# Attention and two dense layers on one core: queries loaded by whole tiles, values by pairs of heads, and all attention loads on ScalarE's queue

## The chip, the cores and the metric

The program runs on one core of a Trainium2 chip. A core has five engines that each work through their own list of instructions in order: TensorE (PE, matrix products), VectorE (DVE), ScalarE (ACT), GpSimd (POOL) and SyncE (SP, which here only starts transfers). Transfers (DMA) are started by an instruction of one of these engines and then run by themselves; an instruction that needs the data waits on a semaphore. The metric is the device time of one execution in microseconds (us); less is better. The kernel before takes 687.59 us, the median of three runs (685.85 to 687.65).

## What is computed

```python
def _attn_ref(q, k, v):                     # 2 batches, 8 heads, 576 positions, 64 wide
    scores = scale * np.matmul(q, k.transpose(0, 1, 3, 2))
    kth = np.partition(scores, -top_k, axis=-1)[..., -top_k:-top_k + 1]   # top_k = 32
    scores = np.where(scores >= kth, scores, -1000000000.0)
    attn = np.exp(scores - np.max(scores, axis=-1, keepdims=True))
    attn = attn / (np.sum(attn, axis=-1, keepdims=True) + 1e-09)
    return np.matmul(attn, v)
...
    x = attention, as 1152 tokens x 512
    h = x @ w_in;  x = (max(h, 0) + log1p(exp(-|h|))) @ w_out           # layer 0, 512 -> 2048 -> 512
    h = x @ w_in2; x = (max(h, 0) + alpha * min(h, 0)) @ w_out2         # layer 1, the same sizes
```

Inputs are float32, but the weights reach the device as 64-bit numbers, which the kernel turns into float32 itself.

## The kernel before

**Tiles.** The 1152 tokens are nine tiles of 128. `CHUNKS` (L35) groups them as [3, 4], [5, 6, 7] and [8, 0, 1, 2]. Tile 4 lies across the two batches, so it has two parts. For each tile and each of its 8 heads there is one row of attention work, 72 in all (`rows`, L377).

**One row of attention.** `scores` (L408) works on a pair of heads: PE forms the products of a query tile `q` with the keys `ks` (L430) and ACT copies them from PSUM to `s`, half a row at a time (L435). `topk` (L445) finds the 32 largest of 576 scores on DVE with four MAX (`best`, L439) and three MATCH_REPLACE (`strike`, L442), then masks and exponentiates with ACT and POOL (L459 to L485; the mask may go to DVE, L478). `flip` (L487) transposes the result on PE, and `values` (L506) multiplies by the values `v` on PE. `finish` (L558) scales a finished tile; its last step writes `xh`, the input of layer 0.

**Weights.** 32 units of 128 x 1024 numbers are turned from 64 bits into float32 by `convert` (L311): a load of 1 MB into `cr` (L317, two buffers), two DVE instructions (L320 and L325), one ACT instruction (L327), four POOL additions (L331) and a store of 512 KB to a scratch tensor `ws` (L334). `fetch` (L352) loads a unit back when a layer needs it (L359).

**Layers.** `Layer.up` (L611) forms `ph` from the tile inputs (L623 for the chunks worked in plain float32, L594 to L596 for the others, as three products of parts), `down` (L655) accumulates `pa` (L671, or again L594 to L596). Between them, for layer 0, ACT and DVE form `g`; its last step is the SCALAR_TENSOR_TENSOR of L638. `ph` has two buffers, so the third `ph` needs the first `g` to be done. Chunk 0 (tiles 3 and 4) goes through layer 0, then layer 1, while attention for chunk 1 is still under way, and so on.

**What sets the order.** Nothing is issued where it is written. Each piece of work is handed to a `Planner` (L97) with an engine, an assumed length and a due time; `order` (L143) lists all pieces engine by engine, always the piece with the earliest due time among those whose inputs are ready by its own estimate. The due times come from constants (`PACE`, `ROWS_DUE`, `AHEAD`, `LOAD_LEAD` and others, L48 to L66). The engines then run these lists in order.

**Loads for attention.** All transfers are in SP's list. Keys come as one load of 288 KB for two heads (`prepare_k`, L397), values as one load of 160 KB for one head (`prepare_v`, L406), and queries as one load of 64 KB for a tile and a pair of heads (L418, inside `scores`). A load into a buffer that is still read waits for PE; everything behind it in SP's list waits too. Transfers also take turns on eight completion semaphores: the ninth cannot be issued before the first has landed, and so on.

Of the kernel before, what the change touches and what calls it, by code (L numbers as in the profile page):

```python
# [19 lines left out]
P = 128  # L20
# [14 lines left out]
CHUNKS = [[3, 4], [5, 6, 7], [8, 0, 1, 2]]  # L35
RING = 4
# [5 lines left out]
QB = 6  # L42
KB = 5
VB = 10
# [3 lines left out]
SPARE = [-17033.9, 2009.0, 903.3]  # L48
MASK_SPARE = [24031.0, 784.7, -18754.5]
# [5 lines left out]
T0 = 229.4  # L55
VALUES = 1.35
SCORES = 0.69
PACE = [1433.1, 1301.1, 6152.8, 6484.8, 326.6, 8896.4]
ROWS_DUE = [(-1910.7, -760.0), (978.8, 846.5), (2800.8, 12532.4)]
EARLY_DUE = [-2160.8, -143.0, 2538.2]  # L60
LOAD_LEAD = 3880.4
FETCH_LEAD = [364.0, 1458.3, -965.3]
EARLY = 24
DIRECT_LEAD = 9718.0
RAW_LEAD = 2408.7
AHEAD = {'scores': [1943.9, 1871.5, 6694.5], 'mask': [46.7, -1169.1, 345.0], 'flip': [12526.4, 4276.2, 25384.6], 'values': [-301.3, 947.9, -2654.2], 'chain': [9471.3, 6009.7, -3110.2], 'split': [1852.9, -2106.4, -15053.3], 'edge': [5637.9, -646.3, 560.8]}  # L66
MASKS = [['act'], ['act'], ['act']]
NATIVE = {(0, 0), (1, 0)}
# [199 lines left out]
def topk_attention_moe_kernel(ctx: ExitStack, tc: tile.TileContext, q, k, v, w1, w2, w3, w4, alpha, out):  # L268
# [4 lines left out]
    plan = Planner()  # L273
    op = plan.op
# [19 lines left out]
    begins = [T0 + sum(PACE[:i]) for i in range(2 * len(CHUNKS))]  # L294
# [6 lines left out]
    def moe_due(ci, layer, j):  # L301
        n = 2 * ci + layer
        return begins[n] + PACE[n] * j / FJ

# [6 lines left out]
    def convert(unit, due):  # L311
# [22 lines left out]
        op("SP", 0.45, due, lambda: nc.sync.dma_start(z, f().bitcast(F32)), reads=[f], writes=[f"ws{nm}"],  # L334
# [65 lines left out]
    def prepare_v(b, h, ci, due):  # L400
        if (b, h) in vst:
# [104 lines left out]
    def values(i):  # L506
# [5 lines left out]
        for b, _, _ in spans(t):  # L512
            prepare_v(b, h - 1, ci, due)
            prepare_v(b, h, ci, due)
# [4 lines left out]
        parts = [((vst[b, h - 1], vst[b, h]), c0, w) for b, c0, w in spans(t)]  # L519

        def products():
            for vts, c0, w in parts:
                o = h // 2 * P + c0
                for c in range(5):
                    for half, vt in enumerate(vts):
                        block = (c + 5 * half if c < 4 else 4) * P + c0
                        nc.tensor.matmul(av()[half * D:(half + 1) * D, o:o + w], vt()[:, c, :], pt[:, block:block + w],
                                         start=c == 0, stop=c == 4)

        op("PE", VALUES * len(parts), due, products, reads=[*pts] + [vt for vts, _, _ in parts for vt in vts], writes=[av],  # L530
# [4 lines left out]
    def features(name, bufs, ci, layer):  # L535

        n = len(CHUNKS[ci]) * P
# [60 lines left out]
    class Layer:  # L598
# [3 lines left out]
        def __init__(self, layer, ci):  # L602
            self.layer, self.ci, self.tiles = layer, ci, CHUNKS[ci]
# [4 lines left out]
            self.turned = layer == 0 and ci == len(CHUNKS) - 1 and not self.native  # L608
# [46 lines left out]
        def down(self, j):  # L655
# [40 lines left out]
            if self.layer == 0:  # L696
# [123 lines left out]
```

## Time and profile before

| | us |
|---|---|
| median of three runs | 687.59 |
| lowest and highest run | 685.85, 687.65 |
| the profiled execution, its own time | 689.61 |
| its span, first to last instruction | 687.7 |
| PE busy | 620.6 (90%) |
| DVE busy | 544.3 (79%) |
| ACT busy | 485.3 (71%) |
| POOL busy | 359.6 (52%) |

The rest of the page divides the span into 40 slices, lists the chain of work that ended last, the costliest groups of instructions, and the transfers. PE's share of the span grows from about half in the first fifth to nearly all of the time afterwards; DVE's is highest in the first half. A busy share over the whole span therefore hides that different engines are full at different times, and the tables by stretch have to be read beside it.

### The profile page before, as it was taken

How to read it: one execution, taken by the hardware profiler on the slowest of the kernel's cores; microseconds unless marked ns; L12 is line 12 of the kernel's file. 1: busy time of each engine (PE TensorE's matmuls, PEld its weight loads, DVE VectorE, ACT ScalarE, POOL GpSimd, SP SyncE). 2: the span in 40 equal slices, each digit the busy share in tenths (PEclk: the TensorE clock that was granted, in tenths of full speed). 3: DMA queues.
4: the chain of work that ended last, by engine and by line, in shares of the span. 5: the costliest groups of instructions: out<-in, count | busy, mean ns of one | idle time of the engine just before them, and what ended most of it. 6: DMA issues, size and time to landing. Idle time of an engine off the chain costs nothing.

```text
span 687.7 us, 10318 instructions
## 1 busy us (share of the span) xinstructions
PE 620.6 (90%) x3432; PEld 463.7 (67%) x3432; DVE 544.3 (79%) x1024; ACT 485.3 (71%) x975; POOL 359.6 (52%) x393
## 2 busy tenths in 40 slices
PE   5746545699999999999999999999999999999997
PEld 3424434466666566568877778878888888788885
DVE  4999999999999899999999999989545544554442
ACT  3877678698869778878888888788675655533431
POOL 0575666565575469766987677868411112121120
PEclk9686655699999999999999999999999999999999
DMA  8877667778978883842332312122142232313121
GB/s 286 283 250 232 196 215 216 239 238 269 305 266 309 248 271 108 269 148 84 123 108 92 106 50 93 62 93 92 62 168 95 91 112 72 121 63 123 61 92 61
DMA packets 34324, 109.59 MB, mean 159 GB/s; under 512 B 3936, under 2 KB 12128, under 8 KB 30176
## 3 DMA queue, kind: packets, MB, share of 16 engines
q1 hardware_dynamic: 34272, 108.94, 47.7%
q8 instruction: 27, 0.44, 0.3%
q14 instruction: 25, 0.20, 0.1%
HBM read 89.79 MB, written 19.14 MB: 158 GB/s over the span
## 4 chain that ended last, share of the span: by engine, by line
PE 67%; DVE 12%; DMA 7%; POOL 5%; issue 4%; ACT 4%; SPq 1%; POOLq 0%; DVEq 0%; ACTq 0%
PE ph L594 8%; PE pa L594 8%; PE pa L596 8%; PE pa L595 8%; PE ph L596 8%; PE ph L595 8%; DMA cr<-in_w_dram 6%; PE pa L671 5%; DVE m L439 4%; PE pss L430 4%; DVE r L442 4%; PE ph L623 4%; PE pp L497 3%; POOL cx L331 3%; DVE cr L325 2%
## 5 line engine op out<-in xcount | busy, mean ns | idle before, releaser
L439 DVE MAX8 m<-r 128x8 f32<-128x576 f32 x216 | 156.2, 747 | 0.4
L481 POOL TENSOR_TENSOR e<-s,e 128x288 f32<-128x288 f32 x144 | 122.6, 862 | 40.1 <-ACT e L476 28.4
L331 POOL TENSOR_TENSOR cx<-cx,cr 128x256 int32<-128x256 int32 x128 | 98.8, 792 | 83.3 <-ACT cr L327 61.5
L343 POOL TENSOR_TENSOR w<-w 128x512 fp32r<-128x512 f32 x68 | 92.3, 1367 | 79.3 <-ACT w L349 75.6
L442 DVE MATCH_REPLACE8 r<-m,r 128x576 f32<-128x576 f32 x144 | 106.4, 741 | 0.0
L343 POOL TENSOR_TENSOR gl<-g,gh 128x384 fp32r<-128x384 f32 (+1 forms) x40 | 46.4, 1160 | 100.6 <-ACT gh L651 100.4
L430 PE MATMUL pss<-ks,q 64*128 64x288 f32 x320 | 75.7, 531 | 19.7 <-ACT s L435 11.9
L327 ACT ACTIVATE cr<-cr 128x1024 int16<-128x1024 uint32 x32 | 80.0, 2500 | 17.4 <-DVE cr L325 17.2
L497 PE MATMUL pp<-ident,e 128*128 128x128 f32 x288 | 48.4, 301 | 34.6 <-ACT e L483 21.9
L349 ACT CAST w<-w 128x1024 fp32r<-128x1024 f32 x64 | 66.9, 1045 | 11.1 <-DMA w<-ws 10.9
L497 PEld LDWEIGHTS pp<-ident,e 128*128 128x128 f32 x288 | 37.1, 153 | 52.7 <-ACT e L483 26.6
L430 PEld LDWEIGHTS pss<-ks,q 64*128 64x128 f32 x320 | 35.5, 219 | 48.8 <-ACT s L435 19.3
L594 PE MATMUL pa<-w,gh 128*128 128x512 f32 x160 | 66.9, 418 | 0.0
L435 ACT COPY s<-pss 128x288 f32<-128x288 f32 x144 | 52.0, 406 | 19.6 <-PE pss L430 15.6
L595 PE MATMUL pa<-w,gl 128*128 128x512 f32 x160 | 63.3, 396 | 0.0
L596 PE MATMUL pa<-w,gh 128*128 128x512 f32 x160 | 63.2, 395 | 0.0
L483 ACT ACTIVATE e<-e,nb 128x576 f32<-128x576 f32 x72 | 55.6, 772 | 9.0 <-POOL e L481 9.0
L344 DVE TENSOR_TENSOR w<-w 128x512 fp32r<-128x512 f32 x60 | 45.1, 787 | 18.6 <-ACT w L349 18.6
L638 DVE SCALAR_TENSOR_TENSOR g<-ph,g 128x256 f32<-128x256 f32 (+2 forms) x48 | 26.6, 554 | 42.1 <-ACT g L637 40.9
L439 DVE MAX8 m<-s 128x8 f32<-128x576 f32 x72 | 53.0, 746 | 8.2 <-ACT s L435 8.0
L442 DVE MATCH_REPLACE8 r<-m,s 128x576 f32<-128x576 f32 x72 | 53.4, 741 | 0.0
L644 DVE SCALAR_TENSOR_TENSOR g<-g,rest,ph 128x256 f32<-128x256 f32 (+2 forms) x48 | 29.2, 608 | 30.4 <-ACT g L642 28.3
(127 smaller groups left out, 1389.2 us busy)
## 6 DMA issues: line engine op xcount, KB each, us to landing
w<-ws SPq DMA_DIRECT2D x88, 512.0 KB, 3.3
cr<-in_w_dram SPq DMA_DIRECT2D x32, 1024.0 KB, 7.4
ws<-cx SPq DMA_DIRECT2D x32, 512.0 KB, 7.6
v<-in_v_dram SPq DMA_DIRECT2D x24, 160.0 KB, 4.3
ks<-in_k_dram SPq DMA_DIRECT2D x12, 288.0 KB, 4.3
q<-in_q_dram SPq DMA_DIRECT2D x40, 64.0 KB, 4.1
out_dram<-o SPq DMA_DIRECT2D x9, 256.0 KB, 2.0
al<-in_alpha_dram SPq DMA_DIRECT2D x1, 8.0 KB, 2.8
```

The source lines that it names most:

```text
L327: op("ACT", ACT_LOW, due, lambda: nc.scalar.activation(raw().bitcast(I16)[:, :, 2], low(), AF.Copy, scale=2.0 ** -29), reads=[f], writes=[ ...
L331: op("POOL", on_pool(cs.stop - cs.start), due, lambda cs=cs: nc.gpsimd.tensor_add(f().bitcast(I32)[:, cs], f().bitcast(I32)[:, cs], high() ...
L343: lambda cs=cs: nc.gpsimd.tensor_sub(lo()[:, cs], x()[:, cs], hi()[:, cs].bitcast(F32)),
L349: op("ACT", on_act(WIDE), due, lambda: nc.scalar.copy(w()[:, 0, :], x()), reads=reads, writes=[w])
L430: nc.tensor.matmul(pss[n](), qr()[n * D:(n + 1) * D, :], ks()[n * D:(n + 1) * D, cs], start=j == 0, stop=j == len(qk) - 1)
L439: op("DVE", on_dve(n), due, lambda: nc.vector.max(out=out(), in_=x()), reads=reads, writes=writes)
L442: op("DVE", on_dve(n) + 0.067, due, lambda: nc.vector.match_replace(out=out(), in_to_replace=found(), in_values=x(), imm_value=LOWEST), re ...
L481: op("POOL", on_pool(HS), due - AHEAD["mask"][ci], lambda cs=cs: nc.gpsimd.tensor_sub(e()[:, cs], s()[:, cs], e()[:, cs]), reads=[s], writ ...
L497: nc.tensor.transpose(pp()[:, c * P:(c + 1) * P], e()[:, c0 + c * P:c0 + (c + 1) * P], ident)
L594: nc.tensor.matmul(acc, ah, b_l, start=first, stop=False)
L595: nc.tensor.matmul(acc, a_l, bh, start=False, stop=False)
L596: nc.tensor.matmul(acc, ah, bh, start=False, stop=last)
```

## The change

Queries are loaded for a whole tile at once (four pairs of heads, 256 KB, ten loads in place of forty, two buffers in place of six). Values are loaded for a pair of heads (320 KB, twelve loads in place of twenty-four, five buffers of double size in place of ten). Keys keep their twelve loads. All 34 of these loads are issued by ACT; SP keeps the weights, the scratch stores, the fetches and the output. The new `STORER` is SP as before, and `TOGETHER` with three groups of one chunk leaves the layers as they were. The planner's constants have new values, so that the order of work on every engine is another one.

```diff
+LOADER = 'ACT'
+STORER = 'SP'
+ISSUE = {"SP": 0.45, "ACT": 0.45, "POOL": 1.0}
-QB = 6
+QB = 2
-VB = 10
+VB = 5
-T0 = 229.4
+T0 = 30.2
-PACE = [1433.1, 1301.1, 6152.8, 6484.8, 326.6, 8896.4]
+PACE = [1198.9, 591.1, 6130.8, 6026.0, 276.5, 3112.4]
...
-        op("SP", 0.45, due + AHEAD["scores"][ci] - LOAD_LEAD, lambda: nc.sync.dma_start(ks(), k[b, pair]), writes=[ks],
-           move=P * S * 4)
+        op(LOADER, ISSUE[LOADER], due + AHEAD["scores"][ci] - LOAD_LEAD, lambda: loader.dma_start(ks(), k[b, pair]),
+           writes=[ks], move=P * S * 4)
...
-        vst[b, h] = vt = buf("v", VB, [P, 5, D], F32, f"v{b}{h}")
-        op("SP", 0.45, due + AHEAD["values"][ci] - LOAD_LEAD / 2, lambda: nc.sync.dma_start(vt(), v[b, h]), writes=[vt], move=P * 5 * D * 4)
+        vst[b, pair] = vt = buf("v", VB, [P, 2, 5, D], F32, f"v{b}{pair}")
+        op(LOADER, ISSUE[LOADER], due + AHEAD["values"][ci] - LOAD_LEAD / 2, lambda: loader.dma_start(vt(), v[b, pair]),
+           writes=[vt], move=P * 10 * D * 4)
+
+    def prepare_q(t, n, ci, due):
+        if (t, n) in qst:
+            return
+        qst[t, n] = qr = buf("q", QB, [P, H // 2, P], F32, f"q{t}_{n}")
+        op(LOADER, ISSUE[LOADER], due + AHEAD["scores"][ci] - LOAD_LEAD, lambda: loader.dma_start(
+            qr(), q[:, NT if n else t]), writes=[qr], move=P * H // 2 * P * 4)
...
-            qr = buf("q", QB, [P, P], F32, f"q{t}{pair}{n}")
-            op("SP", 0.45, due + AHEAD["scores"][ci] - LOAD_LEAD, lambda n=n, qr=qr: nc.sync.dma_start(
-                qr(), q[:, NT if n else t, pair]), writes=[qr], move=P * P * 4)
-            qk.append((qr, kst[b, pair]))
+            prepare_q(t, n, ci, due)
+            qk.append((qst[t, n], kst[b, pair]))
...
-                        nc.tensor.matmul(pss[n](), qr()[n * D:(n + 1) * D, :], ks()[n * D:(n + 1) * D, cs],
+                        nc.tensor.matmul(pss[n](), qr()[n * D:(n + 1) * D, pair, :], ks()[n * D:(n + 1) * D, cs],
...
-            prepare_v(b, h - 1, ci, due)
-            prepare_v(b, h, ci, due)
+            prepare_v(b, h // 2, ci, due)
...
-        "v": vp.reshape(B, H, 5, P, D).transpose(0, 1, 3, 2, 4),
+        "v": vp.reshape(B, H // 2, 2, 5, P, D).transpose(0, 1, 4, 2, 3, 5),
```

What the new order is shows in two places.

**ACT's list, from its start.** In a name, the digits say which part it is: `s30` is tile 3, head 0; `cr010` is a weight unit of layer 0; `ks00` and `v00` are batch 0 and pair 0; `q4_0` is tile 4. DMAHW0 to DMAHW7 are the eight completion semaphores. Before, from the second instruction on:

```order
L282 ACT_TABLE_LOAD
L435 COPY s30_139<-pss300_127 128x288 [waits PE_49]
L435 COPY s31_141<-pss310_129 128x288 [waits PE_49]
L435 COPY s30_139<-pss301_145 128x288 [waits PE_49]
L435 COPY s31_141<-pss311_147 128x288 [waits PE_49]
L459 ACTIVATE nb30_171<-m30_161 128x1 [waits DVE_49]
```

Now, after the table load and the loads of `ks00`, `q3_0`, `ks01`, `ks02` and `ks03`, which wait for nothing:

```order
L421 DMA q4_0_124<-in_q_dram 128x512 [waits DMAHW0_49]
L405 DMA ks10_126<-in_k_dram 128x576 [waits DMAHW1_49]
L414 DMA v00_128<-in_v_dram 128x640 [waits DMAHW2_49]
L414 DMA v01_130<-in_v_dram 128x640 [waits DMAHW3_49]
L414 DMA v02_132<-in_v_dram 128x640 [waits DMAHW4_49]
L414 DMA v03_134<-in_v_dram 128x640 [waits DMAHW5_49]
L414 DMA v10_136<-in_v_dram 128x640 [waits DMAHW6_49]
L335 ACTIVATE cr000_109<-cr000_109 128x1024 [waits DVE_49]
L294 ACTIVATE rest_70<-al_69 128x16
L335 ACTIVATE cr010_113<-cr010_113 128x1024 [waits DVE_49]
L449 COPY s30_158<-pss300_147 128x288 [waits PE_49]
L449 COPY s31_161<-pss310_149 128x288 [waits PE_49]
```

Twelve loads and two weight conversions now stand ahead of the first copy of scores. DMAHW0 is the semaphore of `cr000` and DMAHW2 that of `cr010`, the first two loads in SP's list, which in the kernel before came behind eleven loads of keys and queries. DVE's list begins with L328 and L333 for `cr000` and then for `cr010`, and the first MAX is fifth; before, it was first.

**DVE's list where layer 0 begins.** `xh0` is the input of layer 0 for chunk 0, `g00_0` its first result between the two products. Before:

```order
L581 TENSOR_TENSOR xh0_694<-pav4__748,xn4_1160 128x4x128
L442 MATCH_REPLACE r55_1171<-m55_1133,s55_1082 128x576
L320 TENSOR_SCALAR cx007_1178<-cr007_1114 128x1024
L439 MAX m55_1133<-r55_1171 128x8
L325 TENSOR_SCALAR cr007_1114<-cr007_1114 128x1024
L442 MATCH_REPLACE r55_1171<-m55_1133,r55_1171 128x576
L439 MAX m52_1048<-r52_1056 128x8
L439 MAX m55_1133<-r55_1171 128x8
L442 MATCH_REPLACE r54_1217<-m54_1145,s54_1079 128x576
L442 MATCH_REPLACE r55_1171<-m55_1133,r55_1171 128x576
L320 TENSOR_SCALAR cx017_1229<-cr017_1153 128x1024
L638 SCALAR_TENSOR_TENSOR g00_0_1219<-ph00_0_1174,g00_0_1219 128x256
```

Now:

```order
L594 TENSOR_TENSOR xh0_626<-pav4__711,xn4_1118 128x4x128
L333 TENSOR_SCALAR cr017_1069<-cr017_1069 128x1024
L453 MAX m55_1100<-r55_1120 128x8
L456 MATCH_REPLACE r54_1145<-m54_1111,s54_1056 128x576
L456 MATCH_REPLACE r55_1120<-m55_1100,r55_1120 128x576
L453 MAX m54_1111<-r54_1145 128x8
L453 MAX m55_1100<-r55_1120 128x8
L456 MATCH_REPLACE r54_1145<-m54_1111,r54_1145 128x576
L456 MATCH_REPLACE r55_1120<-m55_1100,r55_1120 128x576
L453 MAX m54_1111<-r54_1145 128x8
L652 SCALAR_TENSOR_TENSOR g00_0_1169<-ph00_0_1138,g00_0_1169 128x256
```

From the list's start to this first `g00_0`, DVE had 84 MAX, 64 MATCH_REPLACE, 16 of L320 and 15 of L325; now it has 86 MAX, 65 MATCH_REPLACE, 16 of L328, 16 of L333 and one mask (L492). On PE the same work stands ahead of the first `ph` of layer 0 in either list: 60 score products, 81 transposes, 120 products with values and 16 that spread the sums. The same holds once more where the first `ph` of chunk 1 begins: 108 score products, 184 transposes and 240 products with values are behind it in either list.

## Rows read from the trace of the kernel before

**Rows 1.** The page: busy tenths in 40 equal slices of the span.

```profile
PE   5746545699999999999999999999999999999997
DVE  4999999999999899999999999989545544554442
```

**Rows 2.** By stretch: start:end length, busy time of engines, clock, DMA share, GB/s.

```profile
0.00:17.20 17.20, 9.02 (x26) 5.60 (x26) 7.73 (x16) 6.52 (x14) 0.70 (x6) 0.97 0.85 286
17.20:141.60 124.40, 73.28 (x492) 49.81 (x492) 120.59 (x236) 93.63 (x183) 78.04 (x97) 0.66 0.72 230
141.60:310.00 168.40, 164.87 (x878) 107.72 (x879) 159.44 (x317) 139.01 (x293) 108.73 (x133) 1.00 0.74 245
310.00:600.00 290.00, 289.94 (x1682) 233.66 (x1681) 219.87 (x407) 213.80 (x443) 158.25 (x151) 1.00 0.28 95
600.00:687.70 87.70, 83.47 (x358) 66.89 (x356) 36.69 (x53) 32.32 (x47) 13.90 (x8) 1.00 0.24 84
...
8.00:13.00 5.00, 4.80 (x14) 2.61 (x12) 2.90 (x7) 2.19 (x7) 0.00 (x0) 1.00 0.97 333
```

**Rows 3.** Timeline where layer 0 begins: start, length, engine, work, [idle before, releaser].

```profile
132.97 0.69 DVE L581 TENSOR_TENSOR xh<-pav__748,xn 128x512 f32<-128x512 f32 x1 [0.30 <-ACT xn L578]
...
141.12 0.41 DVE L638 SCALAR_TENSOR_TENSOR g<-ph,g 128x256 f32<-128x256 f32 x1
...
141.59 1.99 PE L623 MATMUL ph<-xh,w 128*128 128x256 f32 x8 [1.34 <-DVE g L638]
```

**Rows 4.** Timeline of the first 20 us.

```profile
0.74 0.39 SPq L397 DMA_DIRECT2D ks<-in_k_dram  x1
...
5.92 0.90 SPq L317 DMA_DIRECT2D cr<-in_w_dram  x2
...
6.51 1.61 DVE L439 MAX8 m<-s 128x8 f32<-128x576 f32 x2 [6.51 <-ACT s L435]
...
13.77 0.69 DVE L320 TENSOR_SCALAR cx<-cr 128x1024 uint32<-128x1024 uint32 x1 [2.87 <-DMA cr<-in_w_dram]
```

**Rows 5.** Transfers issued near 6 us and near 93 us: KB, us to landing.

```profile
cr<-in_w_dram SPq DMA_DIRECT2D x2, 1024.0 KB, 8.8
...
cr<-in_w_dram SPq DMA_DIRECT2D x1, 1024.0 KB, 5.7
```

**Rows 6.** ACT's groups from 0 to 20 us: xcount, busy us, mean ns.

```profile
L327 ACT ACTIVATE cr<-cr 128x1024 int16<-128x1024 uint32 x2 | 5.0, 2484 | 4.7 <-DVE cr L325 4.7
L435 ACT COPY s<-pss 128x288 f32<-128x288 f32 x12 | 4.4, 406 | 4.9 <-PE pss L430 4.9
```

**Rows 7.** DVE's groups from 0 to 141.1 us (L478: 0 to 297).

```profile
L439 DVE MAX8 m<-r 128x8 f32<-128x576 f32 x62 | 44.6, 744 | 0.0
L442 DVE MATCH_REPLACE8 r<-m,r 128x576 f32<-128x576 f32 x42 | 30.9, 738 | 0.0
L325 DVE TENSOR_SCALAR cr<-cr 128x1024 uint32<-128x1024 uint32 x15 | 12.9, 860 | 0.0
...
L478 DVE TENSOR_SCALAR e<-s,m 128x576 f32<-128x576 f32 x5 | 2.9, 587 | 0.0
```

**Rows 8.** DVE's waits, 17.2 to 141, then 141 to 310 us.

```profile
DVE cx L320 <- DMA cr<-in_w_dram: 3.5, 3, 1.6
...
DVE cx L320 <- DMA cr<-in_w_dram: 4.9, 5, 2.0
```

**Rows 9.** What SP's list waited for, 0 to 297 us: total, times, longest.

```profile
SPq L418 <- PE pss L430: 38.7, 11, 7.6
...
SPq L397 <- PE pss L430: 18.0, 6, 7.1
...
SPq L406 <- PE pav__748 L527: 6.2, 2, 5.1
```

**Rows 10.** What PE waited for, 0 to 141 us.

```profile
PE pss L430 <- DMA q<-in_q_dram: 3.8, 1, 3.8
...
PE pss L430 <- DMA ks<-in_k_dram: 0.7, 1, 0.7
```

More of the change, by code (lines that the diff above doesn't have):

```diff
@@ L47 @@
 OB = 4
-SPARE = [-17033.9, 2009.0, 903.3]
-MASK_SPARE = [24031.0, 784.7, -18754.5]
+SPARE = [-7022.5, 1525.8, -3032.5]
+MASK_SPARE = [945.1, 705.4, -504.7]
 CXB = 3
@@ L273, in topk_attention_moe_kernel @@
     plan = Planner()
+    loader, storer = ({"SP": nc.sync, "ACT": nc.scalar, "POOL": nc.gpsimd}[x] for x in (LOADER, STORER))
     op = plan.op
@@ L293, in topk_attention_moe_kernel @@
     first_row = [sum(len(c) for c in CHUNKS[:i]) * H for i in range(len(CHUNKS) + 1)]
-    begins = [T0 + sum(PACE[:i]) for i in range(2 * len(CHUNKS))]
+    among = {ci: group for group in TOGETHER for ci in group}
+    passes = [(layer, ci) for ci in range(len(CHUNKS)) for layer in (0, 1) if not layer or among[ci][-1] == ci]
+    begins = {p: T0 + sum(PACE[:i]) for i, p in enumerate(passes)}
+    paces = dict(zip(passes, PACE))
     def row_due(i):
@@ L301, in moe_due @@
     def moe_due(ci, layer, j):
-        n = 2 * ci + layer
-        return begins[n] + PACE[n] * j / FJ
+        return begins[layer, ci] + paces[layer, ci] * j / FJ
     mats = {0: (w1, w2), 1: (w3, w4)}
@@ L518, in values @@
         pt = pts[0].tile
-        parts = [((vst[b, h - 1], vst[b, h]), c0, w) for b, c0, w in spans(t)]
+        parts = [(vst[b, h // 2], c0, w) for b, c0, w in spans(t)]
         def products():
-            for vts, c0, w in parts:
+            for vt, c0, w in parts:
                 o = h // 2 * P + c0
                 for c in range(5):
-                    for half, vt in enumerate(vts):
+                    for half in range(2):
                         block = (c + 5 * half if c < 4 else 4) * P + c0
-                        nc.tensor.matmul(av()[half * D:(half + 1) * D, o:o + w], vt()[:, c, :], pt[:, block:block + w],
+                        nc.tensor.matmul(av()[half * D:(half + 1) * D, o:o + w], vt()[:, half, c, :], pt[:, block:block + w],
                                          start=c == 0, stop=c == 4)
-        op("PE", VALUES * len(parts), due, products, reads=[*pts] + [vt for vts, _, _ in parts for vt in vts], writes=[av],
+        op("PE", VALUES * len(parts), due, products, reads=[*pts] + [vt for vt, _, _ in parts], writes=[av],
            share=0.5)
@@ L535, in features @@
     def features(name, bufs, ci, layer):
-        n = len(CHUNKS[ci]) * P
+        n = sum(len(CHUNKS[c]) for c in (among[ci] if layer else [ci])) * P
         if (layer, ci) in NATIVE:
@@ L602, in __init__ @@
         def __init__(self, layer, ci):
-            self.layer, self.ci, self.tiles = layer, ci, CHUNKS[ci]
+            self.layer, self.ci = layer, ci
+            self.tiles = [t for c in (among[ci] if layer else [ci]) for t in CHUNKS[c]]
             self.n = len(self.tiles) * P
@@ L607, in __init__ @@
             self.passes = 4 if self.native else 3
-            self.turned = layer == 0 and ci == len(CHUNKS) - 1 and not self.native
+            self.turned = layer == 0 and ci == len(CHUNKS) - 1 and len(among[ci]) == 1 and not self.native
             self.g = {}
@@ L695, in down @@
                 return
-            if self.layer == 0:
-                ys[ci] = [features("y", 1, ci, 1)] * KT
+            group = among[ci]
+            before = sum(len(CHUNKS[c]) for c in group[:group.index(ci)])
+            if self.layer == 0 and not before:
+                ys[group[-1]] = [features("y", 1, group[-1], 1)] * KT
             os = [buf("row", OB, [P, DM], F32, f"o{nm}{ti}") for ti in range(len(self.tiles))]
@@ L709, in down @@
                 if self.layer == 0:
-                    to_features(o, bank("pacc", 3, 512, f"py{nm}{ti}"), ys[ci][0], ti, due)
+                    to_features(o, bank("pacc", 3, 512, f"py{nm}{ti}"), ys[group[-1]][0], before + ti, due)
                 else:
@@ L744, in topk_attention_moe_kernel @@
             attend(first_row[ci + 2] - 1)
-        for layer in (0, 1):
+        for layer in (0, 1) if among[ci][-1] == ci else (0,):
             lay = Layer(layer, ci)
```

23 lines of the change are left out of this document (12 added, 11 removed).

## The prediction, made before the changed kernel was run

> **What bounds the kernel now.** I read the page's 40 slices first. The reader is to see that PE works about half of the time in the first eight slices and nine tenths or more in nearly every slice after them, while DVE is full from the second slice on and thins out from the middle [rows 1]. So the span has two parts, and a mean busy share says nothing of either. The table by stretch sharpens this. From 17.2 to 141.6 us DVE is busy for 120.59 of 124.40 us, at a granted PE clock of 0.66: the first part waits for DVE, and PE's slow clock there costs nothing. From 141.6 us on PE is granted 1.00, the higher of its levels, and idles for only 168.40 - 164.87 = 3.5 us up to 310 us and 0.1 us up to 600 us; the rest of its idle time, 4.2 us, lies in the last stretch [rows 2]. The border is the start of layer 0. The timeline shows it: `xh` of the second tile is written at 132.97, the first `g` at 141.12, and PE, which had waited 1.34 us for that `g`, goes on at 141.59 [rows 3].
>
> From this comes the rule of the sum. PE's work is the same in both kernels, and the lists of both have the same attention work ahead of layer 0 and again ahead of chunk 1. So the end moves by as much as the first `g` moves, less what PE can catch up behind it, which is at most the 3.5 us idle before 310 us.
>
> **The start.** Before, SP issues keys and queries first, from 0.74 us; the two weight loads follow at 5.92. The first MAX stands at 6.51, and DVE later idles 2.87 us for the first weights, so that its idle time at the start is 6.51 + 2.87 = 9.4 us [rows 4]. Now ACT has twelve loads and two conversions (L335) ahead of the first copy of scores. The load of `v00` cannot be issued until `cr010` has landed, since both use one semaphore; the copies, and with them the first MAX, stand behind it. Step by step:
>
> - `cr010` is SP's second instruction, at 0.74 + 0.45 = 1.2 us (0.90 us for two issues [rows 4]). Two weight loads issued together took 8.8 us in the median [rows 5]; the first was awaited until 13.77, 7.85 after its issue at 5.92 [rows 4], so the second took 2 x 8.8 - 7.85 = 9.75. That pair, too, shared the engines with other loads. So `cr010` lands at about 11.0.
> - Five loads of values then go out. No row shows a load on ACT; I take SP's 0.45 each, 2.2 us: 13.2.
> - Two conversions on ACT, 5.0 us [rows 6], and a short instruction on 16 columns that I put at 0.2: 18.4.
> - `s30` is complete with the third copy, 3 x 4.4 / 12 = 1.1 us [rows 6]: the first MAX at 19.5.
>
> Until then DVE has only the four weight instructions, at 0.69 each [rows 4] 2.8 us. It idles 16.7 us, against 9.4 before: **7.3 us lost**. The lower end: a weight load nearly by itself took 5.7 us [rows 5]; with that, and loads that cost ACT nothing, the first MAX stands at 6.9 + 5.2 + 1.1 = 13.2, and 1.0 us is lost. The upper end: all that is queued ahead of the values, two loads of 1024 KB, two of 256 and five of 288, is 4000 KB or 4.1 MB, at the 333 GB/s of 8 to 13 us [rows 2] 12.3 us; the first MAX at 22.0, 9.8 us lost. I take the middle value because its row is two weight loads that were issued together beside other loads, as they are now.
>
> What the rows show so far is one queue, in which the keys land first because they were issued first. The Trainium skill, DMA: Bandwidth & Descriptors, section on queues, rings and completion order, says that each DMA engine takes packets in turn from every queue that has work. By that rule the keys and the weights share from the start, and as a weight packet is larger (8 KB rows here against 2 KB) the weights would get most of the rate: `cr010` would land some 1.5 us earlier and the sum would be about 695 us. No run here shows two such queues yet.
>
> **DVE's list up to the first `g`.** It has 2 MAX more (44.6 / 62 = 0.72 each), one MATCH_REPLACE (30.9 / 42 = 0.74), one weight instruction (12.9 / 15 = 0.86) and one mask (2.9 / 5 = 0.58) [rows 7]: 1.4 + 0.7 + 0.9 + 0.6 = **3.6 us later**. DVE is full there, so all of it lies on the path. Its waits for weights on the way, 3.5 us before [rows 8], I leave as they are: a buffer comes free after ACT and POOL as before, and the positions of the weight instructions in the list are nearly the same. If all of them go, 3.5 us are gained; if they double, 3.5 are lost.
>
> **What is hidden.** The thirty fewer loads of queries and twelve fewer of values save SP's issue time, which nothing waits for: PE waited for queries once, 3.8 us, and for keys once, 0.7, before layer 0 [rows 10], and at the start the copies are now later than either. The first query load is 256 KB in place of 64: under 1 us at 333 GB/s, hidden behind the conversions on ACT. The other 22 loads cost ACT 22 x 0.45 = 9.9 us over the run; ACT idles for 124.40 - 93.63 = 30.8 us in the second stretch and 29.4 in the third [rows 2], so I cost them at nothing. Without that cover each would push a copy or an exponential by 0.45.
>
> **SP's list.** Loads that waited for PE held SP for 38.7 + 18.0 + 6.2 = 62.9 us in the first 297 us [rows 9], with weight loads, stores and fetches queued behind them. That is gone. What it can give is bounded by what DVE waited for weights, 3.5 and 4.9 us [rows 8], and by PE's 3.5 us after 141.6 us, since nothing else waits for SP there. A weight load also needs its buffer back from POOL, which moving the others does not hasten. I count half of PE's idle time before 310 us, **1.8 us back**.
>
> **Sum.** 7.3 + 3.6 - 1.8 = 9.1 us. The profiled execution took 689.6 us and would take 698.7; the median of the runs shown, 687.59, lies 2.0 us below it, which gives 696.7 us. Behind 310 us I count nothing: PE idles for 0.1 us there until 600, and the last 87.7 us have the same work. With all bounds at one side the case reaches from 1.0 + 3.6 - 3.5 - 3.5 = -2.4 (685.2) to 9.8 + 3.6 + 3.5 = 16.9 (704.5).
>
> **Rivals.**
>
> *Two queues feed the start and the weights faster* (ends faster). The two weight loads land as quickly as a single one, ACT issues at no cost, and with SP free DVE no longer waits for weights nor PE for what follows. Then the same sum is 1.0 + 3.6 - 3.5 - 3.5 = -2.4, 685.2 us. For it: 62.9 us of blocked SP time. Against it: the same engines carry the same bytes, at 0.85 busy in the first 17 us [rows 2], and the two conversions of 2.5 us on ACT stand ahead of the copies whatever the loads do. It decides if the first MAX comes before about 13.5 us and the waits for weights vanish; with only one of the two the result is within 0.3% or slower. Chance 0.15 for faster, 0.12 for within 0.3%, which is about what a measurement of this kernel can tell from no change (685.5 to 689.7 us).
>
> *ACT waits in the middle.* The loads that held SP for 62.9 us in 19 waits, 3.3 us each, now hold ACT, with copies of scores, exponentials and transposes behind them; DVE and PE wait for those. ACT has 30.8 us to spare before layer 0 for some 11 such loads, 2.8 us each. Above that mean, DVE starves: at 3.3 us each, 11 x 0.5 = 5.5 us more, and about half of that again before 310 us: 696.7 + 8 = 705 us. Against it: the list puts such a load where the planner believes the buffer to be free, and ACT, unlike SP, reaches it late because it has other work. Chance 0.13.
>
> *The queries and values arrive in fewer, larger loads and that by itself gains.* At most the 4.5 us that PE waited for such data [rows 10], none of it on DVE's path; it is within the low end above and has no chance of its own. That the change does not do what it says is excluded by the lists: 34 loads stand in ACT's.
>
> **How the numbers follow.** Forecast 0.60, at 696.7 us; ACT waits 0.13, at 705; both are slower, 0.73 together. Within 0.3%: 0.12. Faster: 0.15, at 685. The range reaches down to 685.0, which leaves out most of the faster case, and up to 706.0, which takes in the upper bound of the forecast and the middle of the ACT case.
>
> **What would show it.** Right: the first MAX near 19.5 us, with `v00` issued on ACT when `cr010` lands and two ACT conversions ahead of the first copy; the first `g` near 152 us; DVE full between; PE at clock 1.00 and without idle time from there on; the last 380 us as long as before. Wrong start: a first MAX before 14 us. Wrong rule: a first `g` that is late by 11 us and an end that is not, which would mean that PE was not full after 141.6 us although it is shown busy. ACT case: long waits of ACT's loads for PE between 40 and 300 us, and DVE idle for `s`.

## The result and the profile after

The changed kernel takes 694.05 us, the median of four runs (693.04 to 696.98), against 687.62 for the kernel before in the same comparison: 6.4 us more, a ratio of 1.0099 with a 95% interval of 1.0077 to 1.0122. The prediction was 696.7 us, slower. The profiled execution took 696.98 us, and its span is 694.8 us.

The page's slices first, as in [rows 1]:

```profile
PE   1665745499999999999999999999999999999997
DVE  1999998998998999999997999999645544453442
```

The picture is the same but for the first slice, in which DVE and PE now stand nearly still. By stretch, with the columns of [rows 2]:

```profile
0.00:17.20 17.20, 2.67 (x8) 1.62 (x9) 2.78 (x4) 6.75 (x7) 3.63 (x11) 1.00 0.86 334
17.20:141.60 124.40, 73.14 (x471) 48.71 (x470) 120.70 (x240) 90.38 (x182) 74.78 (x95) 0.68 0.65 221
141.60:310.00 168.40, 163.69 (x904) 107.61 (x904) 157.39 (x310) 136.77 (x282) 101.31 (x121) 0.99 0.70 237
310.00:600.00 290.00, 289.85 (x1667) 233.14 (x1666) 223.21 (x414) 221.05 (x462) 162.07 (x157) 1.00 0.28 98
600.00:694.80 94.80, 90.72 (x388) 72.29 (x386) 40.30 (x59) 35.28 (x52) 13.89 (x8) 1.00 0.24 84
```

In the first 17.2 us DVE is busy for 2.78 us; before it was 7.73. From there on both kernels show the same two regimes: DVE full, then PE full. The timeline of the start tells what DVE waited for (compare [rows 4]):

```profile
0.74 0.86 SPq L325 DMA_DIRECT2D cr<-in_w_dram  x2
0.77 0.39 ACTq L405 DMA_DIRECT2D ks<-in_k_dram  x1
1.19 0.45 ACTq L421 DMA_DIRECT2D q<-in_q_dram  x1
...
6.36 0.69 DVE L328 TENSOR_SCALAR cx<-cr 128x1024 uint32<-128x1024 uint32 x1 [6.36 <-DMA cr<-in_w_dram]
...
9.42 2.27 ACTq L414 DMA_DIRECT2D v<-in_v_dram  x5
9.42 0.69 DVE L328 TENSOR_SCALAR cx<-cr 128x1024 uint32<-128x1024 uint32 x1 [1.64 <-DMA cr<-in_w_dram]
...
9.70 2.26 PE L444 MATMUL pss<-ks,q 64*128 64x288 f32 x6 [9.70 <-DMA q<-in_q_dram]
...
11.73 2.46 ACT L335 ACTIVATE cr<-cr 128x1024 int16<-128x1024 uint32 x1 [9.72 <-DMA ks<-in_k_dram]
...
14.01 2.48 ACT L335 ACTIVATE cr<-cr 128x1024 int16<-128x1024 uint32 x1
...
16.24 1.08 ACT L449 COPY s<-pss 128x288 f32<-128x288 f32 x3
...
17.35 0.76 DVE L453 MAX8 m<-s 128x8 f32<-128x576 f32 x1 [6.51 <-ACT s L449]
```

This is the predicted chain link by link: the second weight unit lands and DVE starts on it at 9.42; at that same time ACT can issue the first load of values; five loads, two conversions and three copies follow, and the first MAX stands at 17.35 us, where 19.5 was expected. DVE is idle for 6.36 + 1.64 + 6.51 = 14.5 us until then. The start of layer 0, to be read against [rows 3]:

```profile
139.82 0.69 DVE L594 TENSOR_TENSOR xh<-pav__711,xn 128x512 f32<-128x512 f32 x1
...
147.06 0.40 DVE L652 SCALAR_TENSOR_TENSOR g<-ph,g 128x256 f32<-128x256 f32 x1
...
148.62 1.89 PE L637 MATMUL ph<-xh,w 128*128 128x256 f32 x8
```

The first `g`, expected near 152 us, is 147.06 - 141.12 = 5.9 us later than before, and the end of the span 694.8 - 687.7 = 7.1 us. DVE's groups up to the first `g` (columns of [rows 7], then idle time before them and its releaser) show where its part of this comes from:

```profile
L453 DVE MAX8 m<-r 128x8 f32<-128x576 f32 x64 | 46.1, 748 | 0.1
L456 DVE MATCH_REPLACE8 r<-m,r 128x576 f32<-128x576 f32 x43 | 31.8, 743 | 0.0
...
L453 DVE MAX8 m<-s 128x8 f32<-128x576 f32 x22 | 16.1, 749 | 7.0 <-ACT s L449 7.0
L333 DVE TENSOR_SCALAR cr<-cr 128x1024 uint32<-128x1024 uint32 x16 | 12.0, 753 | 0.1
L328 DVE TENSOR_SCALAR cx<-cr 128x1024 uint32<-128x1024 uint32 x16 | 11.6, 722 | 10.4 <-DMA cr<-in_w_dram 10.4
...
L492 DVE TENSOR_SCALAR e<-s,m 128x576 f32<-128x576 f32 x1 | 0.9, 927 | 0.1
```

The kernel before had this row for the first of the two weight instructions, beside that of L325 in [rows 7]:

```profile
L320 DVE TENSOR_SCALAR cx<-cr 128x1024 uint32<-128x1024 uint32 x16 | 13.1, 821 | 6.3 <-DMA cr<-in_w_dram 6.3
```

The two MAX, one MATCH_REPLACE, one weight instruction and one mask more are there, but the weight instructions together take 12.0 + 11.6 = 23.6 us in place of 13.1 + 12.9 = 26.0, with one more of them. By the table of stretches cut at each kernel's first `g`, DVE is busy for 129.0 us in place of 127.8. So the account up to the first `g` is: 14.5 us idle at the start against 9.4 (+5.1), 1.2 us more work, 0.3 us less waiting, together 6.0. Behind it the rest of the span is 1.1 us longer (547.7 against 546.6). One wait of PE stands out there, at 224 to 227 us, which the kernel before does not have:

```profile
PE py L561 <- ACT o L723: 2.8, 1, 2.8
```

A weight load came late: DVE stood still for 2.48 us until 222.31 us before it could start on that unit, ACT's conversion waited 2.34 us for DVE, and the copy that PE needed stood behind the conversion. From 220 to 240 us PE's mean granted clock was 0.91; in the 20 us before and after it was 1.00.

### The profile page after: what moved, and what is told of

The parts are those of the page before. It is cut to its first block, busy times and chain, and to the rows that moved or that the text cites. A ratio compares the mean times of both kernels' runs of the same rounds, so it can differ in the third digit from the quotient of the medians.

```text
span 694.8 us, 10229 instructions
## 1 busy us (share of the span) xinstructions
PE 620.1 (89%) x3432; PEld 463.4 (67%) x3432; DVE 544.4 (78%) x1024; ACT 490.2 (71%) x981; POOL 355.7 (51%) x390
## 4 chain that ended last, share of the span: by engine, by line
PE 71%; DVE 14%; ACT 4%; DMA 4%; issue 4%; POOL 2%; ACTq 0%; SPq 0%; POOLq 0%; DVEq 0%
PE ph L607 8%; PE pa L607 8%; PE pa L609 8%; PE pa L608 7%; PE ph L608 7%; PE ph L609 7%; PE ph L637 6%; DVE m L453 6%; PE pa L685 6%; DVE r L456 6%; PE pss L444 4%; DMA cr<-in_w_dram 4%; PE pp L511 3%; ACT cr L335 3%; DVE cr L333 1%
## 5 line engine op out<-in xcount | busy, mean ns | idle before, releaser
L351 POOL TENSOR_TENSOR w<-w 128x512 fp32r<-128x512 f32 x64 | 87.7, 1386 | 72.2 <-ACT w L357 67.2
L444 PE MATMUL pss<-ks,q 64*128 64x288 f32 x320 | 77.8, 543 | 31.2 <-ACT s L449 13.0
L351 POOL TENSOR_TENSOR gl<-g,gh 128x384 fp32r<-128x384 f32 (+1 forms) x37 | 42.7, 1155 | 99.9 <-ACT gh L665 99.9
L335 ACT ACTIVATE cr<-cr 128x1024 int16<-128x1024 uint32 x32 | 79.8, 2499 | 17.9 <-DMA ks<-in_k_dram 9.7
L352 DVE TENSOR_TENSOR w<-w 128x512 fp32r<-128x512 f32 x64 | 48.7, 794 | 22.2 <-ACT w L357 22.0
```

The source lines that it names most:

```text
L335: op("ACT", ACT_LOW, due, lambda: nc.scalar.activation(raw().bitcast(I16)[:, :, 2], low(), AF.Copy, scale=2.0 ** -29), reads=[f], writes=[ ...
L351: lambda cs=cs: nc.gpsimd.tensor_sub(lo()[:, cs], x()[:, cs], hi()[:, cs].bitcast(F32)),
L444: nc.tensor.matmul(pss[n](), qr()[n * D:(n + 1) * D, pair, :], ks()[n * D:(n + 1) * D, cs], start=j == 0, stop=j == len(qk) - 1)
```

## The experiments

Each is compared with runs of the kernel before on the same chip; these medians lie between 686.8 and 688.0 us. The runs of one kernel spread over up to 7.6 us, and the profiled execution may be a high or a low one: where it matters, its own time is given.

### What the start is worth

**The change with its loads on SP**, its lists otherwise kept.

```diff
-lambda: loader.dma_start(ks(), k[b, pair])
+lambda: nc.sync.dma_start(ks(), k[b, pair])
...
```

> The changed kernel with every list in the same order, except that the 34 loads stand on SP instead of ACT, at the same places in the overall order. Theory (the start decides, the rest passes through): ACT's first weight conversion no longer waits behind twelve loads; it starts at about 7.8 us instead of 11.7, the first copy of scores follows the second conversion near 13 us, the first MAX stands near 14 instead of 17.4, the first g moves from 147.1 to about 144, and the time falls by 3 us to about 691. Rival 1 (loads on SP hold up weights and fetches again, as in the kernel before): the start gains 3 us and PE and DVE lose them again behind it, 694 or more. Rival 2 (what ACT issues costs nothing at the start either, the weights set it): 694, first MAX unchanged.

Measured: 691.92 us (690.44 to 693.66), ratio 1.0056 (1.0035 to 1.0078). The first MAX stands at 13.5 us, the first `g` at 143.6. The queue alone costs 3.5 us of the first `g`, as the theory had it, and 2.1 of the median, where the intervals of the two ratios just touch. The two conversions still stand ahead of the copies, and the rest of the loss remains.

**The change with one row of ACT's list moved**: the second conversion behind the first four copies.

```diff
...
+        place[marks[units[1]] + 3] = place[firsts[0] + 5] + 0.1
...
```

> The changed kernel, with one row of ACT's list moved: the second conversion stands behind the first four copies of scores. Theory (what ACT has ahead of the first copies is a part of the loss): first MAX at 15 in place of 17.35 us; the third weight unit, issued at 17.12 and landed at 23 to 25, then takes some of it back at DVE's sixteenth row, so first g at 145 to 146 and a median of 692 to 693 us. Rival (the third unit takes all of it back, since nothing brings that load forward): first g at 147, median 694 us.

Measured: 692.44 us (690.30 to 694.98), ratio 1.0078 (1.0054 to 1.0101). First MAX at 15.0 us, first `g` at 145.3: as the theory had it. Against the change the intervals overlap, so the 1.6 us rest on the trace more than on the medians.

**Both at once.**

> The changed kernel with both edits to its start at once: its loads issued by SP at the places of its order, and ACT's second conversion behind the first four copies of scores. Theory (idle time of DVE at the start is on the path, so the two gains, 2.1 us and 1.6 us in the median, add up): ACT's first copy follows the load of the 16 columns at 9.6 us, first MAX at 11, first g at 141 to 142, median 690 to 690.7 us, which leaves about 3 us over the kernel before for the rest of the new order. Rival (one and the same limit stands behind both, the third weight unit or PE's remaining work): first MAX at 11 all the same, first g at 143.5, median 691.5 to 692.5 us.

Measured: 691.88 us (687.86 to 695.42, 12 runs), ratio 1.0058 (1.0035 to 1.0080): no better than the first of the two alone, and what the rival named. The trace shows the moved row at work, with the first copy now behind PE and not behind the conversion:

```profile
7.10 2.48 ACT L337 ACTIVATE cr<-cr 128x1024 int16<-128x1024 uint32 x1 [5.09 <-DVE cr L335]
9.76 0.22 ACT L294 ACTIVATE rest<-al 128x16 f32<-128x16 f32 x1 [0.19 <-DMA al<-in_alpha_dram]
11.04 0.70 ACT L452 COPY s<-pss 128x288 f32<-128x288 f32 x2 [1.06 <-PE pss L447]
```

First MAX at 12.4 us, where 11 was expected, and first `g` at 142.8. DVE's idle time until the first MAX is now 5.64 + 1.85 + 2.09 = 9.6 us, as good as the 9.4 of the kernel before: in this trace the whole loss of the start is gone. The profiled execution, 688.24 us, is the second lowest of the twelve. A full sum of the two gains would be a ratio of about 1.0035, which is the edge of the interval, so the medians speak against it without excluding it; which of the rival's two limits stands behind that, the runs do not tell.

### Loads on ACT in other orders

**The change with the planner's constants of the kernel before**, loads still on ACT.

```diff
-T0 = 30.2
+T0 = 229.4
...
-LOAD_LEAD = 4845.3
+LOAD_LEAD = 3880.4
...
```

> The changed kernel with the planner's constants of the kernel before: loads by whole tiles and pairs, all on ACT. Its lists begin as the changed kernel's do, with twelve loads and two conversions ahead of the first copy, and have 140.0 us of DVE work ahead of the first g by the durations of the trace, against 139.4 in the changed kernel and 135.8 before. Theory (start and DVE's list decide, constants only through them): first MAX near 17.4, first g near 147.5, 694 to 695 us. Rival (the new constants are what costs or gains): as before, near 688, if they cost; 697 or more, if they gain.

Measured: 693.79 us (693.57 to 694.50), ratio 1.0084 (1.0069 to 1.0099), first MAX at 17.4 and first `g` at 147.6. The new constants are not the cause: with the old ones the planner again puts both weight units first. It does so when it is told that ACT loads: with the same constants and the loads planned for SP (further below), keys and queries come first again.

**The kernel before with its 76 loads on ACT**, in its own order.

```diff
-lambda: nc.sync.dma_start(ks(), k[b, pair])
+lambda: nc.scalar.dma_start(ks(), k[b, pair])
...
```

> The kernel before with its 76 small loads of keys, queries and values issued by ACT at the places where its order has them. Theory (ACT's issue time and its waits for landings at the start are the price, the middle is nearly free): the first MAX at 11 to 13 us in place of 6.5, but no wait for weights; 3 us more idle time, median 690 to 692 us. Rival (loads that wait hold ACT's copies in the middle as they held SP): DVE starves for scores between 20 and 140 us, first g at 150 or later, median 696 us or more. The distance to the change tells what merging the loads buys on this queue.

Measured: 691.63 us (691.16 to 692.84), ratio 1.0063 (1.0039 to 1.0087). The first MAX is at 13.64 us, somewhat later than expected, and the first `g` at 143.6. DVE then does not wait for the first weights, since they start at once on SP. So ACT's queue costs 2.1 us of the median in the one order and 4.8 in the other; in the other only 2.5 us of it are at the first `g`, and the rest is not explained. In this order the 76 small loads on ACT cost no more than the 34 large ones of the change (691.63 against 694.05), and no copy of ACT's waits for one of them after 20 us: what merging buys depends on the order.

**The change with its loads cut into the old sizes**, same lists.

```diff
-lambda: loader.dma_start(vt(), v[b, pair])
+lambda: [loader.dma_start(vt()[:, n], v[b, pair][:, n]) for n in range(2)]
...
-            qr(), q[:, NT if n else t])
+            qr()[:, g], q[:, NT if n else t, g]) for g in range(H // 2)]
```

> The changed kernel with the same lists and buffers, but each load of queries issued as four of 64 KB and each of values as two of 160 KB, as the kernel before has them: 76 loads on ACT in place of 34. Theory (issue time on ACT at the start is on the path, in the middle it is hidden): 11 loads more ahead of the first copies at 0.33 to 0.45 us each, some of it while ACT waits for landings anyway: first MAX 2 to 5 us later, at 19.5 to 22, first g at 149 to 152 and a median of 696 to 699 us. Rival 1 (issue time is hidden behind the landing of the second weight unit): 694 us as the change. Rival 2 (the 31 loads in the middle cost ACT 11 us that it has not): first MAX as above and 700 us or more.

Measured: 710.01 us (708.34 to 710.16), ratio 1.0327 (1.0307 to 1.0348); first MAX at 22.3 us, first `g` at 161.8. The start is as expected, but the sum is 16 us and not 2 to 5: the second rival's time. ACT's list in the middle:

```profile
94.33 6.75 ACTq L421 DMA_DIRECT2D q<-in_q_dram  x8
101.12 0.40 ACT L449 COPY s<-pss 128x288 f32<-128x288 f32 x1 [6.10 <-DMA q<-in_q_dram]
```

Eight loads of queries in a row hold ACT for 6.75 us, where eight issues at a median of 0.45 are 3.6, and DVE's MAX at 101.55 us waited 4.45 us for the copy behind them. DVE also waits 4.1 us for weights after the start, where the change waits 2.4. At 159.53 us four more query loads hold ACT for 1.79 us between two steps of the first `g`, which DVE awaits for 2.96. With 4.9 us at the start these make 14.0 of the 14.7 us by which the first `g` is later than the change's. This is waiting of ACT in the middle, to which the prediction gave a chance of 0.13, though the trace shows it for loads as such and not for PE. In the change's order, merging keeps it out; that small loads on ACT need not cost this, the run before this one shows.

### An earlier first `g`

**The planner told that SP loads**, with the old constants and then with the new ones.

```diff
-LOADER = 'ACT'
+LOADER = 'SP'
```

With the old constants:

> Loads by whole tiles and pairs, but on SP, with the constants of the kernel before: the sizes alone. Its lists begin as those of the kernel before, keys and queries first, and have 135.6 us of DVE work ahead of the first g against 135.8. Theory: first MAX near 7, first g near 141, 687.5 us, no change; the difference to the kernel with the same constants and the loads on ACT, 6 to 7 us, is the price of the queue. Rival (DVE's list up to chunk 1 decides, which has 8 us more work ahead of its first g than before): 692 to 695.

With the new ones:

> The changed kernel with its new constants, planned anew with the loads on SP. Its lists begin with keys, queries and values, the first two weights behind them; there are 130.2 us of DVE work ahead of the first g, 5.6 less than before, but 20 us more ahead of the first g of chunk 1. Theory (the end moves with the first g): first MAX near 7, first g near 136, 682 us. Rival (DVE is as full as PE up to 310 us, so that work taken out ahead of layer 0 comes back behind it): PE idles between 142 and 310 us, 688 to 700 us.

Measured: 691.44 us (688.66 to 694.17), ratio 1.0057 (1.0038 to 1.0076), and 698.00 us (696.73 to 700.80), ratio 1.0151 (1.0120 to 1.0182). The first MAX is at 7.1 and 7.2 us and the first `g` at 137.4 and 131.4, ten us before that of the kernel before in the second; and both end later. The two theories, 687.5 and 682 us, miss; the rivals, by which the attention work that is left behind the first `g` decides, miss by 0.6 us in the first case and hold in the second. The table by stretch, cut at each first `g`, first of the one and then of the other:

```profile
0.00:137.40 137.40, 79.05 (x491) 53.55 (x493) 126.82 (x247) 97.31 (x188) 79.83 (x104) 0.70 0.70 242
137.40:310.00 172.60, 167.22 (x923) 108.70 (x923) 163.46 (x327) 143.52 (x304) 109.45 (x132) 0.99 0.68 236
```

```profile
0.00:131.40 131.40, 76.18 (x481) 52.48 (x482) 122.07 (x239) 93.35 (x185) 76.99 (x100) 0.70 0.70 237
131.40:310.00 178.60, 167.25 (x900) 106.97 (x899) 170.81 (x339) 146.61 (x309) 106.19 (x131) 0.95 0.71 236
```

The kernel before, in the same cut:

```profile
0.00:141.10 141.10, 82.29 (x517) 55.39 (x517) 127.82 (x249) 99.65 (x196) 78.25 (x103) 0.70 0.73 237
141.10:310.00 168.90, 164.88 (x878) 107.73 (x879) 159.94 (x319) 139.51 (x293) 109.23 (x133) 1.00 0.74 245
```

Layer 0 began earlier by leaving attention behind: PE had done 491 and 481 of its matmuls, not 517. Until 310 us it then idled for 178.60 - 167.25 = 11.4 us in the worse case, at a mean granted clock of 0.95, against 4.0 us at 1.00. DVE was busy for nearly all of that time. So the rule that the end moves with the first `g` needs its condition, the same work ahead of it. For the milder case, with 5.4 us of idle time, that accounts for a part of the loss only. The milder case also divides the change into steps: larger loads on SP, in the lists that the planner makes for them, have a ratio of 1.0057; the same planned for ACT 1.0084; with the new constants, which is the change, 1.0099, the last two within each other's interval.

**The kernel before with four DVE rows moved**, meant to take away its own wait for the first weights.

```diff
...
+    LATER = {(0, 0, 0): (5, 4), (0, 0, 1): (4, 4)}
...
+                place[one] = place[dve[rank[one] + by[part - 1]]] + 0.1 * part
...
```

> The kernel before, with only four rows of DVE's list moved: the instructions on the first two weight units stand three rows (one MAX, two MATCH_REPLACE) later; ACT's, POOL's, PE's and SP's lists are those of before. Theory (DVE's idle time ahead of layer 0 lies on the path, at equal work): of the 2.87 us wait for the first weights 2.1 go, while the units are done as early as before, so nothing else is later; first g at 139, median 2 us below before, 684.7 to 685.5 us if before is 687. Rival (DVE gives the time back at a later wait before layer 0, or PE has as much more idle time behind it): the same median as before within 0.7 us.

Measured: 688.92 us (685.22 to 691.83, 12 runs) against 687.29, ratio 1.0020 (1.0002 to 1.0038). DVE's waits up to 150 us in the profiled execution:

```profile
DVE m L445 <- ACT s L438: 6.5, 1, 6.5
DVE cx L323 <- DMA cr<-in_w_dram: 3.5, 5, 0.9
```

The wait for the first weights is down to 0.47 us and the first `g` is at 138.7, as expected; this execution took 685.22 us. But it is the lowest of the twelve, and the median is 1.6 us above that of the kernel before, with an interval just clear of none: neither the theory's 2 us less nor the rival's 0.7 us. What the other executions lose was not seen.

### A later first `g`

Three kernels move all early weight units in the lists: in the kernel before by three MAX; in the change, with loads on SP and keys first, to the same places; in the change with loads on ACT, to the places of the kernel before, with the first copies of scores ahead of the loads of values. The edit to the weights:

```diff
...
+            place[c + 1] = place[dve[spot]] + 0.1
+            place[c + 2] = place[dve[spot + 1]] + 0.1
+            for kn in range(3, 8):
+                place[c + kn] = place[c + 2] + 0.01 * kn
...
```

> The kernel before, with the two DVE instructions of each early weight unit three MAX later in the list and ACT's and POOL's part behind them; loads, and the attention work ahead of layer 0, as before. Theory (DVE's idle time at the start lies on the path, and the end is the first g plus what PE has left): the 2.87 us for which DVE waited for the first weights go, first MAX still at 6.5 us, first g at 138 instead of 141.1, span 685, median 684.5 us. Rival (the idle time comes back at the third unit, since its buffer is also free later): first g at 140 to 141 and a median of 686.5 to 688 us.

> The changed kernel with all loads on SP, keys and queries ahead of the first weights, and the weights' instructions three MAX later than in the kernel before; everything else in the order of the change. Theory (the whole loss of the change is DVE's idle time at the start): first MAX at 7 us, no wait for the first weights, so 7.5 us less idle time than the change; first g at 139.5, span 687.5, median 686.5 to 688 us. Rival (the rest of the new order costs time as well): first g near 140 and still a median of 690 us or more.

> The changed kernel, loads on ACT as in the change, but in ACT's list the first copies of scores stand ahead of the loads of values and of both conversions, and DVE's weight instructions stand where the kernel before has them. Theory: the first copies wait only for the first queries, which landed at 9.6 us, so the first MAX is at 12 us and DVE then waits for no weights; 2.5 us less idle time than the change, first g at 144.5, median 691.5 us. Rival (the two queues share so that the queries land later still, or the conversions are missed later): first g at 147 and 694 us.

Measured: 709.38 us, ratio 1.0321 (1.0298 to 1.0345); 728.78 us, ratio 1.0601 (1.0561 to 1.0642); 713.51 us, ratio 1.0378 (1.0342 to 1.0415). All three miss theory and rival alike, although the first MAX stood at 6.6, 7.0 and 10.3 us. The edit moves ACT's and POOL's part along as one block, and in the first of the three ACT then waited for POOL's masks; its largest wait up to 160 us is

```profile
ACT e L489 <- POOL e L487: 23.6, 8, 4.7
```

In the kernel before that wait was, up to 141 us:

```profile
ACT e L483 <- POOL e L481: 5.8, 4, 2.4
```

As tests of the start they fail. They are of use for the rule, because they put the first `g` at 160.2, 181.5 and 166.7 us:

| kernel | first `g` | own time of the profiled execution | difference |
|---|---|---|---|
| kernel before | 141.1 | 689.61 | 548.5 |
| kernel before, four DVE rows moved | 138.7 | 685.22 | 546.5 |
| change, both start edits | 142.8 | 688.24 | 545.4 |
| kernel before, loads on ACT | 143.6 | 691.18 | 547.6 |
| change | 147.1 | 696.98 | 549.9 |
| kernel before, weights later | 160.2 | 708.66 | 548.5 |
| change, loads split | 161.8 | 709.98 | 548.2 |
| change, weights later, loads on ACT | 166.7 | 712.53 | 545.8 |
| change, weights later, loads on SP | 181.5 | 732.25 | 550.8 |
| planner for SP, old constants | 137.4 | 691.37 | 554.0 |
| planner for SP, new constants | 131.4 | 698.04 | 566.6 |

The other three lie at 546.0 to 550.1. Over 43 us of first `g` the rest of the execution is the same within 5.4 us, except in the last two. The count of PE's matmuls alone does not set these apart, since the two variants of the change with the weights later have 497 and 495 by their first `g`; what the last one has beside it is PE idle while DVE is still full.

A good part of the 5.4 us can be seen in the traces. The change and its variants with loads on SP and with one conversion later (549.7 to 550.1) all have the wait of PE for ACT's copy near 224 us, 2.8 to 3.0 us long, with a mean granted clock below 1.00 behind it. With both edits (545.4), whose lists there are those of the variant on SP, that wait is 0.4 us and the clock stays at 1.00. The weight load behind it landed in 5.9 us there, and in 9.2 to 9.4 us in the three others. These three slower executions are the highest of their kernels, so this one load is a candidate for what the executions of one kernel differ by; the others were not traced.

None of the kernels tried beats the kernel before.

## Why the prediction was right, and where its sizes were off

**Where the bound lies** held: DVE up to the first `g`, PE behind it.

**The start** was the mechanism, and its term of 7.3 us measured 5.1. The step that failed is the landing of `cr010`: put at 11.0 us, it came at 9.4. The price was taken from two weight loads that shared the engines with more bytes than these: from 5.92 to 16.1 us the kernel before moved 336 GB/s, some 3.4 MB, and the change from 0.7 to 9.42 us 330 GB/s, some 2.9 MB, of which the two weight loads are 2.1 in either. The rate is nearly the same. Five loads took 2.27 us (2.2 predicted), the two conversions with what lies between 4.5 (5.2), the copies 1.1, and DVE's four weight instructions 2.8. With the right landing the first MAX would have been put at 17.9 instead of 19.5; it came at 17.35.

Behind that landing stands how the two queues share. Keys that were issued first on SP, the only queue, landed in 2.7 us in the kernel before:

```profile
ks<-in_k_dram SPq DMA_DIRECT2D x1, 288.0 KB, 2.7
```

In the change the first loads of the two queues read:

```profile
cr<-in_w_dram SPq DMA_DIRECT2D x2, 1024.0 KB, 6.9
ks<-in_k_dram ACTq DMA_DIRECT2D x2, 288.0 KB, 7.2
q<-in_q_dram ACTq DMA_DIRECT2D x1, 256.0 KB, 8.4
```

The first keys took 5.7 us and the second 8.7, so the small loads on their own queue take as long as the 1024 KB on the other. The Trainium skill, DMA: Bandwidth & Descriptors, section on queues, rings and completion order, has the engines take packets in turn from every queue with work; the trace agrees: up to 4 us there were 67 packets of SP's queue and 56 of ACT's, 0.55 MB against 0.13. By that rule the prediction gave 1.5 us less for `cr010` and a sum of about 695, against 1.6 us less and 694.05 measured. That the sum comes so close is partly luck, since the next two terms are off by 2.4 and 2.9 us in opposite directions.

**DVE's list** was counted rightly and priced at 3.6 us, but the busy time grew by 1.2. The step that failed is the price of the weight instructions, taken as unchanged: L325's counterpart went from a mean of 860 to 753 ns, L320's from 821 to 722. The usual one of these did not change (medians of 682 to 691 ns in both kernels); 11 of 31 took more than 0.8 us before and 3 of 32 do now, and each of these ran while POOL was at work on a TENSOR_TENSOR. So the term should have counted how many meet POOL; that POOL is the cause was not tried.

**SP's freed list** was to give 1.8 us back; instead the part behind the first `g` grew by 1.1. PE's idle time between the first `g` and 310 us did not shrink: 4.6 us against 4.0, of which 2.8 are the one wait near 224 us. The step that failed is that less blocking of SP would reach PE. The prediction's own reason against a larger gain fits: a weight load also waits for its buffer. In the first 310 us SP's list now waits for that as follows:

```profile
SPq L325 <- POOL cx L339: 88.0, 26, 7.4
SPq L325 <- ACT cr L335: 61.4, 15, 8.2
```

Before, these were 68.0 us in 21 waits and 16.1 in 7. The two have grown by 65.3 us together, about the 62.9 that were freed: SP's weight loads now wait for POOL and ACT to give a buffer back.

**What was called hidden** held: in the change no load of ACT's took more than half a microsecond between 20 and 310 us, and its longest waits there are for DVE and PE.

**The rivals.** Two queues feeding faster: the keys landed later, not earlier, so no. ACT waiting in the middle: not in the change, but in the variant with split loads, at a higher price than the rival named. Larger loads bringing nothing of their own: right on SP, where with the old constants they ended 4.1 us later (ratio 1.0057). On ACT it depends on the order: in the change's, cutting the loads up costs 16 us, while in the order of the kernel before the small loads cost no more than the large ones do in the change.

**The rule** that the end moves as the first `g` holds for the change. Its condition, equal attention work ahead, was named in the prediction; the two kernels that break the rule do not meet it, but neither, by PE's count, do two that keep it, so the condition is plausible and not shown. In the change PE has 509 matmuls done by the first `g` against 517, which points the way of the 1.1 us, and the wait near 224 us does so too; how much each gives is not shown.

**What stays open.** Taking away idle time at the start gave 2.2 us in the median, not the 4.3 by which the first `g` came earlier with both edits, and the kernel before gained nothing from 2.4 us; the traced executions of these two were among the lowest of their kernels and did follow the rule. So some 4 us of the change's loss were not recovered by any edit. With both edits DVE's idle time at the start is that of the kernel before, and its first `g` still 1.7 us later, with 1.8 us more busy time of DVE ahead of it. Behind it, the traced executions with the late weight load are 4.3 to 4.7 us longer than the one without, 2.4 to 2.6 of it as PE's wait; how often this happens is not known. The larger loads planned for SP with the old constants lose 4.1 us as well. This points to the lists that come with the larger loads; which row of them costs the rest stays open.

## What to carry to other kernels

A queue that is moved to a computing engine is paid for where that engine has something urgent behind its loads: look at the first copies and at every wait for a landing in its list, not at the issue time summed over the run. Loads that share an engine's list with its work cost most where several stand in a row ahead of something that another engine waits for; there, few large ones were better than many small ones. An earlier start of the next stage is a gain only if the stage before is as far along by then, so look at both sides of the border before trusting the milestone.

## What the runs showed of the hardware

The first keys took 2.7 us to land when they led SP's queue, 5.7 us at the head of ACT's queue beside two weight loads on SP, and 5.1 us in SP's queue between the two weight loads: a queue of their own did not make them faster. ACT issued its first load at 0.77 us, while its table load ran from 0.73 to 2.01, so issuing did not wait for that. An issue on ACT took 0.33 to 0.37 us in the median of each kind of load, with 0.67 the longest; SP's issues of weights and of keys took 0.33 to 0.36. One weight load of 1 MB, at the same place of SP's list, took 5.9 us in one traced execution and 9.2 in another.
